# Two steps of one token block placed elsewhere in VectorE's queue, in a fused sketch-attention and SwiGLU kernel

## The chip, the cores and the metric

The kernel runs on one core of one Trainium2 chip. The metric is the device time of one execution in microseconds (us). The engines are named as in the profile: PE is TensorE, DVE is VectorE, ACT is ScalarE, POOL is GpSimd, SP is SyncE (here it only issues DMAs). Each engine works through its own queue of instructions strictly in order.

## What is computed

Two stages, in fp32. First, attention with sketched features, for 4 batches, 4 heads, 1088 tokens and 32 channels:

```
phi(x): a = S1 x, b = S2 x        (8 values each)
        phi = outer product of a and b, 64 features
kv  = sum over tokens of phi(k) v^T ;  z = sum over tokens of phi(k)
out = phi(q) kv / (phi(q) z + 1e-6)
```

The four heads of a token are put side by side (128 channels), which gives x with 4352 tokens. Second, a SwiGLU block with d_ff = 1536:

```
g = x @ w_gate ;  silu = g / (1 + exp(-g)) ;  out = (silu * (x @ w_val)) @ w_out
```

## The kernel before

**Tiling.** x is held transposed (xT, 128 channels on the partitions). The tokens of the first batch form blocks 0 to 2; the other 3264 tokens form seven blocks of up to 480 tokens, numbers 3 to 9, which the code calls `line`. The 1536 hidden columns are 12 pieces of 128. One *unit* is one block by one piece: the two products for gate and value, the SiLU on ACT, and the product of the two, which is stored as a row of `hidden`. Later a *down* step (`down`, L1039) multiplies that row by w_out and adds it up in PSUM; it runs about five units behind. Blocks 3 to 9 give 84 units, numbered y = 0 to 83. Units 0 to 11 are block 3, units 12 to 23 are block 4, and so on.

**Products in parts.** To save PE passes, a product can be made from rounded parts (fp32r) in place of a full fp32 product. For this, the tokens of a block are cut into three parts by `cut_tokens` (L867), in two steps. The first step puts x1 on ACT (L875, a rounded copy) and x0 on POOL (L876, the remainder). The second step puts xd on DVE (L880, made from x0 and x1). The weights are cut likewise by `cut_weights` (L834; its instructions show as L865). Units 0 to 19 cut the value product only; from unit 20 on (`GATES`) both products are cut. `cut_unit` (L959) issues, for one of the units 0 to 19, this: on PE the product with xd (L968) and the full gate product (L970), on ACT a scaled copy (L972), on PE the products with x1 and x0 (L978, L979), on DVE the sum (L980), on ACT the SiLU (L986), and on POOL the product into `hbuf` (L991).

**The order of the work.** There is no scheduler: the order of the source is the order of every queue. The loop over y (L1346 on) issues in each unit: a group of attention work on PE, if y is in `GROUPS`; the unit itself; down steps; the next part of the attention generator (`parts_of`, L1224); a part of the cut gate weights (L865); and at the end the token steps whose time has come (`token_steps`, L1336 to L1340). So a step listed under y stands at the end of unit y in each engine's queue.

**The attention of the later batches** (`attentions`, L608) is spread between the units. For batch index 2, the third batch, the group at unit 4 forms the key sums on PE (L381, L713), and the key sketches of the fourth batch (L347); `fold` (L590) then makes from the sums the third column of the sketch matrix s123 on DVE, in three instructions (L594, L598, L601), and `spread_out` (L718) turns the sums on DVE (L723) and has SP copy them to other partitions and load the next values. The group at unit 6 multiplies the queries with s123 on PE (`query_sketches`, L335) into PSUM banks 6 and 7. After that, DVE makes the features in pieces (L370) and turns them (L758) for the group at unit 20 (L776). The same work for the fourth batch has its fold in the group at unit 20 and its query sketches in the group at unit 22.

**PSUM banks** are taken by the rule "the one whose last taking is longest ago" (`bank`, L113), with bank 3 held for the accumulators of the down steps. A unit takes three of them, so the banks of one unit come round again two to three units later.

Of the kernel before, what the change touches and what calls it, by code (L numbers as in the profile page):

```python
# [19 lines left out]
def kernel(  # L20
# [38 lines left out]
    NCH = Dff // P  # L59
# [807 lines left out]
    def cut_tokens(i, engine=nc.gpsimd):  # L867

        t0, n = blocks[i]
        x = xT[:, t0 : t0 + n]  # L870
        x1, x0, xd = x_parts[i] = [
            apool.tile([P, WB], F32R, tag=tag, name=name, bufs=2)
            for tag, name in (("qb", "x1"), ("dT", "x0"), ("rd", "xd"))
        ]
        nc.scalar.activation(x1[:, 0:n], x, AF.Copy, scale=CUT)  # L875
        engine.tensor_tensor(  # L876
            out=x0[:, 0:n], in0=x, in1=whole(x1[:, 0:n]), op=ALU.subtract
        )
        yield
        nc.vector.scalar_tensor_tensor(  # L880
            out=xd[:, 0:n], in0=whole(x0[:, 0:n]), scalar=-BETA, in1=whole(x1[:, 0:n]),
            op0=ALU.mult, op1=ALU.add,
        )
# [452 lines left out]
    token_steps = {}  # L1336
    for m, i in enumerate(line[1:], 1):
        gen = cut_tokens(i)
        for at in {2: (20, 22), 3: (27, 32), 4: (40, 42)}.get(m, (NCH * m - 10, NCH * m - 9)):
            token_steps.setdefault(at, []).append(gen)  # L1340
    oldest[0] = True
    hold("acc")
# [71 lines left out]
```

## Time and profile before

| | us |
|---|---|
| median of 5 runs | 287.15 (287.02 to 288.04) |
| the profiled execution, whole | 286.94 |
| its span, first to last instruction | 285.1 |
| PE busy in it | 276.5 |
| DVE busy in it | 220.8 |
| unit 4 starts on PE (L968) | 101.89 |
| unit 6 starts on PE (L968) | 108.57 |
| unit 12 starts on PE (L968) | 121.87 |

The granted TensorE clock was 0.999 over the whole span. A profile line gives a line of the kernel (L880), an engine, an operation, and the tiles it writes and reads by their names without numbers (so x1, x0 and a unit's `x` all show as `x`). In a timeline the first two columns are the start and the duration in us; idle time of the engine ahead of the instruction stands in brackets, with the instruction that ended it. In the chain of work the columns are start, duration, and what worked. The records of two PE instructions that follow each other overlap[...].

### The profile page before, as it was taken

The page shows a single profiled execution, that of the slowest core. Times are in us where ns is not written, and L with a number is a line of the kernel's source. Part 1 is how long each engine was busy: PE and PEld are TensorE (multiplying, and loading weights), DVE is VectorE, ACT ScalarE, POOL GpSimd, SP SyncE. Part 2 cuts the span into 40 slices and gives each one's busy share as a digit, 9 for nine tenths or more (in the row PEclk, how much of TensorE's full clock was granted, in tenths as well). Part 3 has the DMA queues.
Part 4 walks back from the last instruction along what each step waited for, and adds up shares of the span by engine and source line. Part 5 has one row for each costly group of instructions (what it writes and reads, how often), then busy time and mean ns, then how long its engine had stood idle before and what let it go on. Part 6 is the DMA issues. An engine that isn't in the chain of part 4 may idle for free.

```text
span 285.1 us, 5583 instructions
## 1 busy us (share of the span) xinstructions
PE 276.5 (97%) x2129; PEld 191.1 (67%) x2129; DVE 220.8 (77%) x324; ACT 175.3 (62%) x316; POOL 177.3 (62%) x173
## 2 busy tenths in 40 slices
PE   7899999999999989999999999999999999999995
PEld 7545565667665656555576677757777777778984
DVE  3997988975495968998657898749889979988741
ACT  3468665723401846655366776867878888877760
POOL 3315432279500886589935787759879789878660
PEclk9999999999999999999999999999999999999999
DMA  6574194222321122000200020001000200010021
GB/s 196 158 220 112 51 273 132 80 78 80 79 44 28 26 80 78 17 0 2 34 18 0 0 36 2 0 2 22 13 0 1 37 0 0 10 28 1 0 35 28
DMA packets 26138, 14.28 MB, mean 50 GB/s; under 512 B 19840, under 2 KB 24192, under 8 KB 26112
## 3 DMA queue, kind: packets, MB, share of 16 engines
q1 hardware_dynamic: 25456, 13.84, 19.1%
q8 instruction: 16, 0.26, 0.4%
q10 hardware_dynamic: 656, 0.10, 0.2%
q14 instruction: 10, 0.08, 0.1%
HBM read 11.41 MB, written 2.23 MB: 48 GB/s over the span
## 4 chain that ended last, share of the span: by engine, by line
PE 89%; DVE 5%; DMA 1%; ACT 1%; POOL 1%; issue 1%; SPq 0%; DVEq 0%; ACTq 0%
PE PS L1060 24%; PE PS L1015 16%; PE PS L968 11%; PE PS L978 10%; PE PS L979 10%; PE PS L970 5%; PE PS L776 2%; PE PS L335 2%; PE PS L347 2%; PE PS L381 2%; DMA kld<-in_k_dram 1%; DVE xd L880 1%; PE PS L1088 1%; PE PS L1055 1%; PE PS L1054 1%; PE PS L1052 1%
## 5 line engine op out<-in xcount | busy, mean ns | idle before, releaser
L991 POOL TENSOR_TENSOR hbuf<-sg,sum 128x480 f32<-128x480 f32 (+1 forms) x83 | 105.3, 1273 | 37.5 <-ACT sg L986 29.2
L980 DVE SCALAR_TENSOR_TENSOR sum<-PS,sum 128x960 f32<-128x960 f32 (+2 forms) x83 | 83.2, 1003 | 26.6 <-ACT sum L972 21.7
L972 ACT ACTIVATE sum<-PS 128x960 f32<-128x960 f32 (+2 forms) x83 | 70.9, 854 | 39.3 <-PE PS L968 37.2
L1060 PE MATMUL PS<-hbuf,wo 128*128 128x480 f32 (+3 forms) x142 | 57.5, 505 | 0.0
L968 PE MATMUL PS<-xd,gphq 128*128 128x480 f32 (+1 forms) x63 | 40.1, 636 | 0.5 <-DVE xd L880 0.5
L978 PE MATMUL PS<-x,w 128*128 128x480 f32 (+1 forms) x83 | 38.5, 464 | 0.0
L986 ACT ACTIVATE sg<-sum 128x480 f32<-128x480 f32 (+1 forms) x63 | 36.6, 581 | 1.0 <-DVE sum L980 0.9
L968 PE MATMUL PS<-xd,wd 128*128 128x480 f32 (+1 forms) x83 | 35.8, 432 | 0.5 <-DVE xd L880 0.5
L1060 PEld LDWEIGHTS PS<-hbuf,wo 128*128 128x128 f32 x142 | 26.6, 189 | 8.4 <-issue 0.9
L979 PE MATMUL PS<-x,wb 128*128 128x480 f32 (+1 forms) x83 | 31.2, 376 | 0.0
L1015 PE MATMUL PS<-xT,wg 128*128 128x384 f32 (+1 forms) x74 | 29.5, 480 | 0.0
L1015 PE MATMUL PS<-xT,wv 128*128 128x384 f32 (+1 forms) x74 | 28.8, 471 | 0.2 <-DVE wv L279 0.2
L1019 ACT ACTIVATE sg<-PS 128x384 f32<-128x384 f32 (+1 forms) x31 | 14.4, 467 | 21.3 <-PE PS L1015 19.6
L968 PEld LDWEIGHTS PS<-xd,wd 128*128 128x128 f32 x83 | 15.7, 189 | 13.1 <-issue 11.4
L978 PE MATMUL PS<-x,graw 128*128 128x480 f32 (+1 forms) x63 | 23.5, 373 | 0.2 <-ACT xT L793 0.2
L979 PE MATMUL PS<-x,graw 128*128 128x480 f32 (+1 forms) x63 | 23.3, 370 | 0.0
L1060 PE MATMUL PS<-hbuf,scaled 128*128 128x480 f32 x48 | 23.2, 564 | 0.0
L1015 PEld LDWEIGHTS PS<-xT,wv 128*128 128x128 f32 x74 | 13.8, 190 | 9.2 <-DVE hbuf L1030 0.9
L968 PEld LDWEIGHTS PS<-xd,gphq 128*128 128x128 f32 x63 | 11.9, 188 | 11.7 <-issue 6.9
L1015 PEld LDWEIGHTS PS<-xT,wg 128*128 128x128 f32 x74 | 13.3, 189 | 9.3 <-issue 1.2
L978 PEld LDWEIGHTS PS<-x,w 128*128 128x128 f32 x83 | 15.6, 188 | 5.8 <-issue 3.4
L979 PEld LDWEIGHTS PS<-x,wb 128*128 128x128 f32 x83 | 15.6, 188 | 5.7 <-issue 4.3
(173 smaller groups left out, 457.1 us busy)
## 6 DMA issues: line engine op xcount, KB each, us to landing
kld<-in_k_dram SPq DMA_DIRECT2D x4, 544.0 KB, 4.2
vld<-in_v_dram SPq DMA_DIRECT2D x12, 144.0 KB, 5.2
qld<-in_q_dram SPq DMA_DIRECT2D x3, 544.0 KB, 3.4
raw<-in_moe_w_out_dram SPq DMA_DIRECT2D x4, 384.0 KB, 4.7
raw<-in_moe_w_gate_dram SPq DMA_DIRECT2D x3, 384.0 KB, 3.7
raw<-in_moe_w_val_dram SPq DMA_DIRECT2D x3, 384.0 KB, 3.5
out_dram<-o SPq DMA_DIRECT2D x16, 60.0 KB, 2.0
vld<-in_v_dram SPq DMA_DIRECT2D x4, 112.0 KB, 4.1
```

Of the source, the lines that this page charges most:

```text
L335: nc.tensor.matmul(ps[32 * a : 32 * a + 32, 96 * (c - c0) : 96 * (c - c0) + 96], qT[:, 4 * c + a, :], s123[:, a : a + H, :, :].rearrange(" ...
L968: nc.tensor.matmul(ds[:, k], wd, xd, start=True, stop=True)
L970: nc.tensor.matmul(g, wg[:, j, :], xT[:, t0 : t0 + n], start=True, stop=True)
L972: nc.scalar.activation(sums, ds, AF.Copy, scale=-1.0 / BETA)
L978: nc.tensor.matmul(ps[:, k], w1, x1, start=True, stop=False)
L979: nc.tensor.matmul(ps[:, k], wb, x0, start=False, stop=True)
L980: nc.vector.scalar_tensor_tensor(out=sums, in0=ps, scalar=1.0 + 1.0 / BETA, in1=sums, op0=ALU.mult, op1=ALU.add)
L986: nc.scalar.activation(sg, sums[:, 0] if both else g, AF.Silu)
L991: nc.gpsimd.tensor_tensor(out=hj[:, 0:n], in0=sg, in1=sums[:, len(ws) - 1], op=ALU.mult)
L1015: nc.tensor.matmul(o[:, 0:n], w[:, j, :], xT[:, t0 : t0 + n], start=True, stop=True)
L1019: nc.scalar.activation(sg[:, 0:n], g[:, 0:n], AF.Silu)
L1060: nc.tensor.matmul(acc[i][:, 0:n], w, hidden[i, j][:, 0:n], **sides)
```

## The change

The steps of block m of `line` were listed under the units 12m - 10 and 12m - 9, unless given by hand. For m = 1, block 4, that is units 2 and 3. The change gives this block a pair by hand, units 3 and 8:

```
 for m, i in enumerate(line[1:], 1):
     gen = cut_tokens(i)
-    for at in {2: (20, 22), 3: (27, 32), 4: (40, 42)}.get(m, (NCH * m - 10, NCH * m - 9)):
+    for at in {1: (3, 8), 2: (20, 22), 3: (27, 32), 4: (40, 42)}.get(m, (NCH * m - 10, NCH * m - 9)):
         token_steps.setdefault(at, []).append(gen)
```

So x1 and x0 of block 4 stand at the end of unit 3 in the queues of ACT and POOL, where they stood at the end of unit 2, and xd of block 4 stands at the end of unit 8 in DVE's queue, where it stood at the end of unit 3, ahead of the fold of the third batch. Block 4 is first used in unit 12. Nothing else is changed.

More of the change, by code (lines that the diff above doesn't have):

```diff
@@ L1338 @@
         gen = cut_tokens(i)
-        for at in {2: (20, 22), 3: (27, 32), 4: (40, 42)}.get(m, (NCH * m - 10, NCH * m - 9)):
+        for at in {1: (3, 8), 2: (20, 22), 3: (27, 32), 4: (40, 42)}.get(m, (NCH * m - 10, NCH * m - 9)):
             token_steps.setdefault(at, []).append(gen)
```

## The prediction

> **What bounds the kernel now.** I read the page first, to see which engine holds the end.
>
> ```profile
> span 285.1 us, 5583 instructions
> PE 276.5 (97%) x2129; PEld 191.1 (67%) x2129; DVE 220.8 (77%) x324; ACT 175.3 (62%) x316; POOL 177.3 (62%) x173
> ```
>
> TensorE (PE) is busy for 97% of the span, and 89% of the chain that ended last is PE. So a change on VectorE (DVE), ScalarE (ACT) or GpSimd (POOL) counts only if it takes away, or adds, a wait of PE. The view of waits, for PE alone, lists all of them; its columns are the total, the number and the longest, in us.
>
> ```profile
> PE PS L335 <- DVE spread L723: 1.1, 1, 1.1
> PE PS L968 <- DVE xd L880: 1.0, 2, 0.5
> ```
>
> The first is one single stall, the longest of the kernel. The chain of work in order of time (start, duration, what) tells what lies behind it.
>
> ```profile
> 103.21 1.17 POOL x L876
> 104.40 1.64 DVE xd L880
> 106.04 0.15 DVE fold L594
> ...
> 106.66 0.25 DVE spread L723
> 106.95 1.69 PE PS L335 x72
> ```
>
> In order: POOL makes x0 of block 4, DVE makes xd of block 4 from it, then come the sums of the third batch (fold, L594 to L601) and the turn of its sums (L723), then PE's query sketches (L335). The fold needs nothing of block 4: it stands behind xd only because DVE works in order. Its own inputs were there long before: PE's last matmul for it (L713) began at 100.17 and took 0.29 us, so about 100.5. DVE's own timeline shows the queue before and after that place (start, us; the idle time in brackets).
>
> ```profile
> 101.14 0.99 DVE L865 TENSOR_TENSOR late<-wg,graw 128x384 f32<-128x384 f32 x1
> ...
> 115.09 0.64 DVE L980 SCALAR_TENSOR_TENSOR sum<-PS,sum 128x480 f32<-128x480 f32 x1
> 115.66 0.94 DVE L370 TENSOR_TENSOR late<-kab 128x768 f32<-128x768 f32 x1
> 116.53 1.56 DVE L865 SCALAR_TENSOR_TENSOR gphq<-late,graw 128x384 fp32r<-128x384 f32 x1
> 118.02 0.64 DVE L980 SCALAR_TENSOR_TENSOR sum<-PS,sum 128x480 f32<-128x480 f32 x1
> ...
> 121.26 0.65 DVE L980 SCALAR_TENSOR_TENSOR sum<-PS,sum 128x480 f32<-128x480 f32 x1
> ...
> 128.55 0.66 DVE L980 SCALAR_TENSOR_TENSOR sum<-PS,sum 128x480 f32<-128x480 f32 x1 [0.16 <-PE PS L979]
> ...
> 130.79 0.66 DVE L980 SCALAR_TENSOR_TENSOR sum<-PS,sum 128x480 f32<-128x480 f32 x1 [0.70 <-PE PS L979]
> ...
> 133.10 0.66 DVE L980 SCALAR_TENSOR_TENSOR sum<-PS,sum 128x480 f32<-128x480 f32 x1 [0.35 <-PE PS L979]
> ```
>
> DVE is idle from 102.13 to 104.40 (2.26 us, released by POOL's x). From unit 6's sum at 110.41 on it has no gap until 128.55. The new place of xd is in this dense stretch: behind L865 at 116.53, ahead of unit 9's sum at 118.02. PE's timeline gives what L335 costs with and without a wait.
>
> ```profile
> 104.91 0.97 PE L1060 MATMUL PS<-hbuf,wo 128*128 128x480 f32 x2
> 106.95 1.69 PE L335 MATMUL PS<-s,qT 128*32 128x96 f32 x72 [1.07 <-DVE spread L723]
> 146.03 0.97 PE L1060 MATMUL PS<-hbuf,wo 128*128 128x480 f32 x2
> 146.93 1.69 PE L335 MATMUL PS<-s,qT 128*32 128x96 f32 x72
> ```
>
> The same pair of lines stands 0.90 us apart in the fourth batch (146.03 to 146.93) and 2.04 here: 1.14 us are stall by this reading, 1.07 by the bracket.
>
> **The change part by part.** No instruction is added or removed: one ACT instruction (x1, L875), one of POOL (x0, L876) and one of DVE (xd, L880) stand later in their queues. The step issues no DMA.
>
> *Taken away: xd ahead of the fold.* After the change DVE comes from L865, which ends at 102.13, straight to the fold. Its four instructions take 0.21, 0.27, 0.22 and 0.24 us; from the fold's start to the transpose's end they took 106.90 - 105.97 = 0.93 us, so they end at about 103.1. PE wants L335 at 104.91 + 0.90 = 105.81. That leaves 2.7 us of cover, so the whole stall goes: -1.07 to -1.14 us, I take -1.1. What is late next at this place? L335 also needs its PSUM banks, 6 and 7. Followed through the code's oldest-bank rule, bank 6 held the third batch's sums (read by the fold and the transpose, 103.1) and bank 7 unit 4's first product (read by ACT at 102.42, 0.57 us long). Its queries were turned by 99.5. Nothing is late.
>
> A rule of the Trainium skill speaks against this cover. "SBUF — State Buffer", section "Who interferes with whom", has it that a VectorE instruction with two SBUF inputs and a GpSimd one that reads SBUF exclude each other for a whole instruction. The row agrees: xd took 1.64 us at 104.40, beside POOL's product at 104.32 (1.21 us), and 0.65 us at 92.36. Of the four, L601 alone has two SBUF inputs; moved to 102.6 it meets POOL's products, which run without a gap from 99.01. By the plain row (0.22) the sums end at 103.1; by the rule, waiting out a whole product, 1.2 us later, 104.3. That is still 1.5 us ahead of 105.81, so both give the same sum.
>
> *Moved: x1 on ACT, from unit 2 to unit 3.* It ran at 98.25 for 0.59 us and now follows the weight part of 99.64, so it ends by about 100.8. ACT was idle for 1.07 us before 101.24, so this costs nothing; without that idle time the copy there would be late by at most 0.6, and PE only sees it through banks reused two units later.
>
> *Moved: x0 on POOL, from behind unit 2's product to behind unit 3's.* 1.2 us each way: unit 3's product is earlier by that, x0 ends at about 105.6 instead of 104.4. Unit 4's product, which POOL started at 107.59 after 2.06 us of idle time, can start then. Cost nothing; its reader xd now stands some 11 us later.
>
> *Moved: SP's queue.* The six copies of spread and the load of the fourth batch's values wait for L723, which comes about 3.8 us earlier. They start near 103 instead of 106.97 and are needed at unit 20 (142): no cost, no gain.
>
> *Added: xd at unit 8's end.* It no longer waits. Queued behind it on DVE are unit 9's sum, two products of the features (L370), L865 and unit 10's sum. Its size lies between 0.65 us (alone) and 1.64 us (beside a POOL product). By the lock rule a whole extra wait is possible; but POOL's last product there (115.88, 1.80 us) ends at 117.68, ahead of xd at 118.02, and the next needs unit 9's sum, which is behind xd. So I take 0.65, with 1.64 for the range. In times of before (all now 1.1 earlier, PE and DVE alike):
> - Unit 12 needs xd at 121.87. It ends at 118.67 (119.66): 3.2 us (2.2) to spare.
> - Unit 13's first product reuses the bank of unit 10's sum. That ends at 121.91 + 0.65 = 122.56 (123.55); PE's record starts at 124.14: 1.6 us (0.6) to spare.
> - The idle gaps of DVE, 0.16, 0.70 and 0.35, swallow 1.21 us by unit 17, and 1.11 us more before unit 19's sum; the transposed features of the third batch, done at 138.76, are later by 0 (0.43) and needed at 140.50.
> - POOL follows its DVE sums. Its gap of 3.68 us ahead of 145.56 takes up the rest, and the products are read by PE five units later.
>
> So it adds no wait of PE; if this cover were gone, xd would cost its own 0.65 to 1.64 us.
>
> *Sum.* The profiled execution took 286.94 us (span 285.1 and 1.84 around it). 286.94 - 1.1 = 285.84. The median of the five runs, 287.15, is 0.21 above it; the same subtraction gives 286.05. After L335 the chain is PE all the way, but for the stall at 153.54 (0.51), which hangs on unit 22's own products and moves along. I add no gain there.
>
> **The rivals.** *Forecast (0.76): 286.05*, from 285.7 to 286.4.
>
> *Part of the gain (0.08): about 286.6.* The sums of the third batch lose more to POOL than one product, or the dense stretch costs 0.5 us at unit 13. For it: L865 took 0.54 us free and 1.0 to 1.3 beside POOL. Against it: 1.5 us spare at the first place and 0.6 at the second, both at their worst ends.
>
> *The wait is only renamed (0.08): 287.15.* If another input of L335 came last at 106.9, removing xd gains nothing. Against it: the bank and the queries above are all done by 104.3.
>
> *Slower (0.08): about 288.1.* The mechanism is VectorE's backlog between unit 8 and unit 13. If xd takes 1.64 and the insertion shifts the phase so that three of the now free instructions behind it also meet POOL (1.0 us each, the difference of xd's two rows), DVE is 4.6 us late at unit 10's sum. Unit 13's first product is held from where the lag passes 2.2 us (124.14 - 121.91), so PE loses 2.4, less the 1.1 won: +1.3, or 288.4; counted from the end of the matmul ahead in the chain (124.67) it is +0.7, or 287.9. I take 288.1. It turns the sign from a lag of about 3.3 us. Against it: only four POOL products fall into these units, and two of the instructions behind xd already pay for one.
>
> **How the numbers follow.** About 0.2% (0.57 us) is what a measurement of this kernel can tell from no change: faster is below 286.58, slower above 287.72. Faster: the forecast and half of the part gain, 0.80. Within: the other half and the renamed wait, 0.12. Slower: 0.08. The range from 285.6 to 286.9 holds the forecast and the part gain, 0.84.
>
> **What would show it.** In the profile after, L335 at unit 6 should have no wait and start 0.90 us after the L1060 ahead of it; the fold should start near 102.2; DVE's idle time before xd should be gone, with xd near 117 and 0.65 us long; unit 13's L968 should show no wait; the stall near 152.4 should still be 0.5; and the span about 284.0. I am wrong if L335 waits for another releaser, or if a new wait of PE for unit 10's sum, for xd at unit 12 or for phT at unit 20 appears.

## The result, and the profile after

The changed kernel takes 285.91 us (median of 24 runs, 285.49 to 287.68), the kernel before 287.12 us beside it. The ratio is 0.9965, with a 95% interval of 0.9954 to 0.9975: between 0.7 and 1.3 us faster. The forecast was 286.05.

The span is the better measure of a step of this size: what lies around it was 1.84 us in the profiled execution of before and 286.86 - 284.0 = 2.9 us in that of after, which hides the gain in the whole time of these two executions. Here are the first lines of the page of the changed kernel.

```profile
span 284.0 us, 5583 instructions
PE 277.0 (98%) x2129; PEld 191.3 (67%) x2129; DVE 220.6 (78%) x324; ACT 175.3 (62%) x316; POOL 177.2 (62%) x173
```

The span fell by 1.1 us; the number of instructions is the same, and no engine but PE changed its busy time by more than 0.2 us. Next, all waits of PE in the changed kernel that the view lists at 0.4 us or more (total, number, longest).

```profile
PE PS L968 <- DVE xd L880: 1.0, 2, 0.5
PE PS L234 <- PEq L1398: 0.9, 1, 0.9
PE PS L490 <- ACT kvz L1208: 0.4, 1, 0.4
```

The wait of L335 for DVE's transpose is gone and no other has come in its place. PE's timeline shows the same pair of lines as before:

```profile
104.95 0.97 PE L1060 MATMUL PS<-hbuf,wo 128*128 128x480 f32 x2
105.85 1.69 PE L335 MATMUL PS<-s,qT 128*32 128x96 f32 x72
```

They are 0.90 us apart, as in the fourth batch; before it was 2.04. DVE's timeline shows both places, the old and the new:

```profile
101.19 0.99 DVE L865 TENSOR_TENSOR late<-wg,graw 128x384 f32<-128x384 f32 x1
102.10 0.21 DVE L594 TENSOR_TENSOR fold<-PS,sq 128x64 f32<-128x64 f32 x1
102.35 0.27 DVE L598 TENSOR_REDUCE w<-fold 128x8 f32<-128x64 f32 x1
102.65 0.68 DVE L601 TENSOR_TENSOR s<-w,own 128x64 f32<-128x64 f32 x1
103.25 0.24 DVE L723 STREAM_TRANSPOSE spread<-PS 128x64 f32<-128x64 f32 x1
...
115.46 1.56 DVE L865 SCALAR_TENSOR_TENSOR gphq<-late,graw 128x384 fp32r<-128x384 f32 x1
116.94 0.65 DVE L880 SCALAR_TENSOR_TENSOR xd<-x,x 128x480 fp32r<-128x480 f32 x1
117.51 0.64 DVE L980 SCALAR_TENSOR_TENSOR sum<-PS,sum 128x480 f32<-128x480 f32 x1
...
120.76 0.64 DVE L980 SCALAR_TENSOR_TENSOR sum<-PS,sum 128x480 f32<-128x480 f32 x1
...
130.26 1.99 DVE L370 TENSOR_TENSOR phq<-qab 128x768 f32<-128x768 f32 x1
```

The fold starts straight behind L865 and its chain ends at 103.49. xd runs at 116.94 for 0.65 us, behind L865 and ahead of unit 9's sum. Two things are longer than I took them: L601 (0.68 us) and the feature product at 130.26 (1.99 us); more on them below.

### The profile page after: what moved, and what is told of

Its sections match the earlier page's. It is cut to its first block, busy times and chain, and to the rows that moved or that the text cites. A ratio compares the mean times of both kernels' runs of the same rounds, so it can differ in the third digit from the quotient of the medians.

```text
span 284.0 us, 5583 instructions
## 1 busy us (share of the span) xinstructions
PE 277.0 (98%) x2129; PEld 191.3 (67%) x2129; DVE 220.6 (78%) x324; ACT 175.3 (62%) x316; POOL 177.2 (62%) x173
## 4 chain that ended last, share of the span: by engine, by line
PE 89%; DVE 5%; ACT 2%; DMA 2%; issue 1%; SPq 0%; DVEq 0%; ACTq 0%
PE PS L1060 24%; PE PS L1015 16%; PE PS L968 11%; PE PS L978 10%; PE PS L979 10%; PE PS L970 5%; PE PS L776 2%; PE PS L335 2%; PE PS L347 2%; DMA kld<-in_k_dram 2%; PE PS L381 1%; DVE sum L980 1%; PE PS L1088 1%; PE PS L1055 1%; PE PS L1054 1%
## 5 line engine op out<-in xcount | busy, mean ns | idle before, releaser
L1060 PE MATMUL PS<-hbuf,wo 128*128 128x480 f32 (+3 forms) x142 | 57.5, 505 | 0.0
L1060 PEld LDWEIGHTS PS<-hbuf,wo 128*128 128x128 f32 x142 | 26.6, 189 | 8.4 <-issue 0.9
L1060 PE MATMUL PS<-hbuf,scaled 128*128 128x480 f32 x48 | 23.2, 564 | 0.0
```

The costliest lines, as they stand in the source:

```text
L1060: nc.tensor.matmul(acc[i][:, 0:n], w, hidden[i, j][:, 0:n], **sides)
```

## The experiments

The theory: PE's stall was a queueing accident. The fold stood on DVE behind xd, and xd waited for POOL's x0. The rivals: moving x1 and x0 makes part of the gain; xd's own time is what costs; unit 8 is a special place; the cover in the dense stretch is thin. All "before" times are medians of runs beside the experiment on the same chip, 287.06 to 287.09 us.

A measure that the start of the kernel doesn't touch helps to read them, since the profiled executions start PE's units up to 2 us apart (the first keys come at a different time, and the first product on them, L347, took 1.49 us in before and 2.19 in the kernel with xd three times). It is the time from the start of unit 4's group (L381) to the query sketches of unit 6 (L335), and from there to the numerators of unit 20 (L776), all starts taken from PE's timelines:

| kernel | steps at | L381 to L335 | L335 to L776 | ratio to before (95%) |
|---|---|---|---|---|
| before | 2, 3 | 7.81 | 33.55 | 1 |
| after | 3, 8 | 6.64 | 33.54 | 0.9965 (0.9954 to 0.9975) |
| xd alone moved | 2, 8 | 6.64 | 33.54 | 0.9952 (0.9935 to 0.9968) |
| x0 alone moved | 3, 3 | 8.00 | 33.54 | 1.0013 (1.0002 to 1.0023) |
| x0 early | 0, 3 | 6.66 | 33.55 | 0.9958 (0.9944 to 0.9972) |
| xd at 4 | 2, 4 | 6.64 | 33.54 | 0.9979 and 0.9947, see below |
| xd three times | 3, 8 | 6.67 | 33.54 | 0.9962 (0.9946 to 0.9978) |
| xd seven times | 3, 8 | 6.64 | 35.81 | 1.0051 (1.0032 to 1.0071) |
| xd at 11 | 3, 11 | 6.63 | 39.94 | 1.0147 (1.0121 to 1.0172) |
| the same, PE kept busy | 3, 11 | 6.63 | 37.05 | 1.0062 (1.0041 to 1.0084) |

**One half of the change at a time.** First xd alone.

```
-... in {1: (3, 8), 2: (20, 22), ...
+... in {1: (2, 8), 2: (20, 22), ...
```

> Steps at units 2 and 8: xd alone is moved, x1 and x0 stay. Queue theory (the fold stood behind xd, and xd behind POOL's x0): the whole gain, about -1.1 us against before, L335 of unit 6 without a wait. Rival (the earlier room on ACT and POOL from moving x1 and x0 makes part of it): clearly less than -1.1, down to 0.

Measured 285.84 us against 287.06, a gain of 1.2; L335 has no wait. The rival falls: moving x1 and x0 is not needed. Then x1 and x0 alone.

```
+... in {1: (3, 3), 2: (20, 22), ...
```

> Steps at units 3 and 3: x1 and x0 alone are moved, xd stays ahead of the fold. Queue theory: x0 ends on POOL at about 105.6 and xd, alone by then, at 106.3, so L335 waits until 107.2: about +0.2 us against before, wait of PE about 1.3. Rival (moving x1 and x0 makes part of the gain): below before by some tenths or more.

Measured 287.41 us against 287.06. By the ratio that is +0.4 us (0.1 to 0.7), by the table's first interval +0.19. PE's two longest waits in this kernel:

```profile
PE PS L335 <- DVE spread L723: 1.3, 1, 1.3
PE PS L968 <- DVE xd L880: 1.0, 2, 0.5
```

The stall became longer, as x0 became later. This half of the change works, by itself, in the wrong direction.

**The wait or the work?** Here xd stays where it was before, ahead of the fold, but its input is made earlier.

```
+... in {1: (0, 3), 2: (20, 22), ...
```

> Steps at units 0 and 3: xd stays where it was in before, ahead of the fold, but x0 is made on POOL three units' products earlier, so that xd need not wait. Queue theory: xd starts at about 102.1, takes 0.65 to 1.64 us, the fold's chain ends at 103.7 to 104.8, ahead of 105.81: about -1.1 us, though xd still stands first. Rival (xd's own time in front of the fold is what costs, not its wait for POOL): the gain is smaller than -1.1 by 0.65 to 1.64 us.

Measured 285.94 us against 287.06. DVE's timeline of this kernel:

```profile
102.41 1.66 DVE L880 SCALAR_TENSOR_TENSOR xd<-x,x 128x480 fp32r<-128x480 f32 x1
103.99 0.21 DVE L594 TENSOR_TENSOR fold<-PS,sq 128x64 f32<-128x64 f32 x1
...
105.14 0.24 DVE L723 STREAM_TRANSPOSE spread<-PS 128x64 f32<-128x64 f32 x1
```

xd is at its slowest (1.66 us), it is still ahead of the fold, and nothing is lost: the chain ends at 105.38, and PE's L335 began at 106.15 without a wait, 0.89 us behind the L1060 ahead of it. So the wait for POOL was the cost; xd's own time fits under the cover.

**Is unit 8 a special place?** xd goes right behind the fold and unit 4's sum.

```
+... in {1: (2, 4), 2: (20, 22), ...
```

> Steps at units 2 and 4: xd right behind the fold and unit 4's sum, ahead of the dense stretch. Queue theory: about -1.1 us against before, the same as the change; xd runs between 105 and 106.5, in DVE's idle time, and nothing of the stretch from unit 8 on is later than in before. Rival (unit 8 is needed): a stall of PE at unit 6 or later, less than -1.1.

The profile had the full gain, span 283.9, but the median was 286.53 against 287.08 (ratio 0.9979, 0.9966 to 0.9992). Since profile and times disagreed, it ran again beside the changed kernel.

> Steps at units 2 and 4 again, beside the changed kernel on the same chip: its profile had the full gain (span 283.9) but its times lay only 0.55 us below before. Queue theory: the same as the changed kernel within 0.2 us. Rival (the place at unit 4 gives part of the gain away): above the changed kernel by 0.3 to 0.6 us.

> The changed kernel again, as the measure for the others of this call: -1.1 us against before.

Measured 285.93 us for xd at unit 4 (ratio 0.9947, 0.9929 to 0.9966) and 286.02 for the changed kernel (0.9955, 0.9937 to 0.9973), against 287.09. The two are the same. The first median was high because of what lies around the span, over 2.2 us in 9 of its 22 runs (2 of 34 of before): the median of their spans, 284.15, was 1.15 below that of before. Unit 8 has no merit of its own.

**How thin is the cover in the dense stretch?** The changed kernel, with xd of block 4 written several times:

```
+        for _ in range(3 if i == 4 else 1):     # 7 in the second
             nc.vector.scalar_tensor_tensor(out=xd[:, 0:n], ...
```

> The changed kernel, with xd of block 4 written three times at unit 8 (the same values), so DVE's lag at unit 10's sum is about 1.95 us in place of 0.65. Spare time as reckoned (1.6 us left at unit 13's bank, 3.2 at unit 12): no new wait of PE, still -1.1 us against before. Rival (the cover in the dense stretch is thinner than reckoned): a new wait of PE of up to 1.3 us.

Measured 285.99 us against 287.08, and no new wait of PE: two more instructions on DVE, 1.3 us of them, cost nothing. From the first xd to unit 9's sum it was 1.94 us in this trace.

> The changed kernel, with xd of block 4 written seven times at unit 8 (the same values): a lag of about 4.55 us at unit 10's sum. Backlog theory (PE is held from a lag of 2.2 us on): PE loses 1.8 to 2.4 us, in units 12 and 13: +0.7 to +1.3 us against before. Rival (other slack takes it up, such as idle time of DVE in units 15 to 19): nearer to -1.1.

Measured 288.82 us against 287.08, by the ratio +1.5 us (0.9 to 2.0). The waits of PE in this kernel (its lines are one further on: L969 is the unit's first product, L981 the sum):

```profile
PE PS L969 <- DVE sum L981: 1.8, 2, 1.1
PE PS L969 <- DVE xd L881: 1.0, 2, 0.5
```

The first line is new: units 12 and 13 wait for the banks of the sums of units 9 and 10. In the table PE loses 35.81 - 33.54 = 2.27 us, within the 1.8 to 2.4 expected, at 4.72 us from the first xd to unit 9's sum. So the rival that would have made this change slower is real, and needs a lag of more than 1.9 us, where xd alone causes about 0.6.

**As late as it can stand.**

```
+... in {1: (3, 11), 2: (20, 22), ...
```

> Steps at units 3 and 11: xd as late as it can stand. Backlog theory (DVE has no gap here, so the place inside the stretch matters): xd follows unit 11's sum and the dot of the queries, ends at about 123.9, and unit 12's first product, wanted at 120.8, waits 3.1 us: about +2.0 us against before. Rival (DVE has time enough anywhere once the fold is ahead): -1.1 us.

Measured 291.02 us against 287.06: +4.0, twice what was expected. The wait itself came out as reckoned, 3.14 us at unit 12. PE's timeline shows what came on top of it:

```profile
119.18 0.96 PE L970 MATMUL PS<-xT,wg 128*128 128x480 f32 x2
...
124.52 0.77 PE L968 MATMUL PS<-xd,wd 128*128 128x480 f32 x1 [3.14 <-DVE xd L880]
125.08 1.80 PE L970 MATMUL PS<-xT,wg 128*128 128x480 f32 x2
125.95 1.33 PE L978 MATMUL PS<-x,w 128*128 128x480 f32 x1
...
131.34 0.97 PE L1060 MATMUL PS<-hbuf,wo 128*128 128x480 f32 x2
```

The same two products L970 take 0.96 us ahead of the wait and 1.80 behind it. A view of stretches agrees (the length, then the busy us of PE, PEld (PE's weight loads), DVE, ACT and POOL with counts, then the granted clock, the DMA share and GB/s):

```profile
116.00:121.00 5.00, 5.00 (x17) 2.73 (x15) 5.00 (x7) 2.98 (x6) 2.21 (x2) 1.00 0.00 0
121.00:125.00 4.00, 0.86 (x2) 0.48 (x2) 3.43 (x5) 0.00 (x0) 3.93 (x3) 0.86 0.00 0
125.00:129.00 4.00, 4.00 (x8) 2.01 (x7) 1.12 (x3) 1.14 (x2) 0.97 (x2) 0.50 0.00 0
129.00:133.00 4.00, 4.00 (x12) 2.32 (x10) 2.51 (x3) 1.57 (x3) 2.85 (x3) 0.79 0.00 0
133.00:137.00 4.00, 4.00 (x14) 2.35 (x13) 2.52 (x5) 1.85 (x4) 4.00 (x4) 1.00 0.01 2
```

The granted clock is 0.50 from 125 to 129, and full again from 133. To tell this from other costs of the stall, PE was given 16 small products to do while it waits, in the kernel with xd at unit 11.

```
+        if y == 12:
+            keep_warm(16, w=480, ps=ds[:, 0])
         for k, (_, _, wd) in enumerate(parts):
             nc.tensor.matmul(ds[:, k], wd, xd, start=True, stop=True)
```

> The kernel with xd at unit 11, and 16 small bf16 products (480 columns each) put on PE ahead of unit 12's first product, written into a bank that this product overwrites: they fill the 3.1 us in which PE waited for xd. Clock theory (the loss of 4.0 us against before, twice what was expected, is the wait of 3.4 us less the 1.1 won, plus a granted clock of 0.50 in the 4 us behind the wait): no dip of the clock, about +2.3 us against before. Rival (the extra time is in waits of DVE and POOL behind the stall): still +3.5 to +4.

Measured 289.3 us against 287.09, by the ratio +1.8 us (1.2 to 2.4), by the medians +2.2. The clock stayed at 1.00 in all three stretches from 121 to 133, of which this is the middle one:

```profile
125.00:129.00 4.00, 4.00 (x15) 2.35 (x13) 2.51 (x5) 2.29 (x4) 2.25 (x3) 1.00 0.00 0
```

Unit 12's first product starts as late as without the small products (124.56 for 124.52), but the clock is not the same: by the table the two profiled executions differ by 39.94 - 37.05 = 2.9 us, the medians of the two sets of runs, on two chips, by 1.7.

**The same accident in two other places.** The changed kernel still has two waits of PE for an xd, of 0.5 us each. One is block 5's, at unit 24, behind unit 22's sum and the dot of the fourth batch.

```
-... in {1: (3, 8), 2: (20, 22), ...
+... in {1: (3, 8), 2: (20, 21), ...
```

> The changed kernel, with block 5's second step at unit 21 in place of 22, so that its xd stands ahead of the wait for unit 22's sum and of the dot of the fourth batch. If the 0.49 us that PE waits at unit 24 for this xd is the same kind of queueing: the wait is gone, about 0.5 us below the changed kernel, -1.6 against before. Rival (the sum of unit 22 or a bank is late as well and takes its place): no gain over the changed kernel.

Measured 285.03 us against 287.08 (ratio 0.9923, 0.9903 to 0.9944). DVE's timeline:

```profile
146.60 1.22 DVE L880 SCALAR_TENSOR_TENSOR xd<-x,x 128x480 fp32r<-128x480 f32 x1
149.48 1.16 DVE L980 SCALAR_TENSOR_TENSOR sum<-PS,sum 128x960 f32<-128x960 f32 x1 [1.66 <-ACT sum L972]
```

xd now lies in what was idle time of DVE, 2.79 us before and 1.66 now. From the fourth batch's query sketches to the start of PE's last record of L1088 it takes 132.79 us where the changed kernel takes 133.55: 0.76 less, for a wait recorded as 0.49 (the lines are at the end). The other is block 3's, at unit 0, behind three feature products. Both of its steps are now issued together.

```
         if begun[0]:
             x_steps = x_steps or cut_tokens(HEAD, nc.vector)
-            next(x_steps, None)
+            run(x_steps)
```

> The kernel with block 5's second step at unit 21, and block 3's two steps issued together, so that its xd stands ahead of the first features of the third batch on DVE instead of behind them. If the wait of PE at unit 0 (0.46 us) is queueing of the same kind: xd ends near 91.1, the wait goes, and the features and POOL's sums behind them end 0.65 us later, at about 99.7, where unit 4's group wants them at 99.4 by then: -0.4 to -0.75 us against that kernel. Rival (the group's sums come late and the wait only moves there): no gain.

Measured 284.1 us against 287.09 (ratio 0.9882, 0.9861 to 0.9903). This is 0.9 us below the kernel with block 5 at unit 21 (medians of two sets of runs, with before at 287.08 and 287.09), a little more than the 0.4 to 0.75 expected. The longest waits of PE in it:

```profile
PE PS L234 <- PEq L1398: 0.9, 1, 0.9
PE PS L490 <- ACT kvz L1208: 0.4, 1, 0.4
```

No wait for an xd is left. With the three moves together the kernel is 3.0 us, 1.2%, faster than before, and no instruction was added or removed.

## Why the prediction was right

**The stall.** The prediction reckoned 1.07 by the bracket and 1.14 from start to start, and took 1.1. The interval from L381 to L335 fell by 7.81 - 6.64 = 1.17 us; part of the profiled span's gain is taken back by PE's first unit starting 0.07 later (93.23 for 93.16). Start to start was the better reading. The cause is shown, not only argued: xd alone moved gives the gain, x0 alone moved makes the stall longer, and x0 made earlier gives the gain with xd in its old place.

**The lock rule at L601.** The row said 0.22, the rule of the Trainium skill ("SBUF — State Buffer", section "Who interferes with whom"), as the prediction used it, up to a whole POOL product more. L601 took 0.68 us. The rule held, but its price was the rest of the product that was running, not a whole one: POOL had begun it at 101.73 and took 1.52 us, so 0.60 us of it were left at 102.65, and L601 ended 0.08 after it, ahead of most of POOL's next product. The same reading gives xd's slow row in before: POOL's product ended at 104.32 + 1.21 = 105.53, and xd 0.51 later. The sum didn't depend on it, since the chain ended at 103.49 and PE wanted it at 105.85.

**xd at unit 8.** Taken at 0.65 with 1.64 as the far end; it took 0.65, at 116.94, after POOL's product had ended (116.60) and before the next began (118.30). Its two neighbours fit the order reckoned, and unit 13's first product had no wait.

**The features of the third batch.** Here a size was off. I had the last transpose (L758) later by 0, at most 0.43, by subtracting DVE's idle gaps. It ended at 137.28 + 0.96 = 138.24; in before it ended at 138.76, which moved by 1.1 is 137.66. So it was later by 0.6. Two feature products (L370, one of them the line at 130.26) took 1.99 us where they had taken 1.38 and 1.40. Here is the first of them in before, in the changed kernel, and with xd at unit 4, with the POOL instruction that it meets (in the third run POOL's instruction began at 129.50 and took 1.28 us).

```profile
130.66 1.28 POOL L540 TENSOR_TENSOR zs<-zs 128x512 f32<-128x512 f32 x1
131.37 1.38 DVE L370 TENSOR_TENSOR phq<-qab 128x768 f32<-128x768 f32 x1
...
130.15 1.29 POOL L540 TENSOR_TENSOR zs<-zs 128x512 f32<-128x512 f32 x1
130.26 1.99 DVE L370 TENSOR_TENSOR phq<-qab 128x768 f32<-128x768 f32 x1
...
130.21 1.38 DVE L370 TENSOR_TENSOR phq<-qab 128x768 f32<-128x768 f32 x1
```

In each, L370 ends 0.81 us after POOL's instruction: it waits for the rest, 0.57 us in before and 1.18 after. DVE had taken up its lag in its idle gaps (131.37 - 1.1 = 130.27, and L370 starts at 130.26), but POOL had not (130.66 - 1.1 = 129.56, and L540 starts at 130.15). With xd at unit 4 nothing is added to the dense stretch, and L370 takes 1.38. So xd's 0.6 us came back by way of POOL. It cost nothing, because L776 was wanted only at 139.39. But idle gaps had been counted as if durations were fixed.

**The slower rival** was sized right as far as the runs go: the prediction let it start at a lag of 2.2 us, the runs place its start between a reckoned lag of 1.95 (free) and one of 4.55 (which costs 2.27). What I didn't name is that unit 12 waits as well, for the bank of unit 9's sum, with 3.2 us to spare in before.

**Readings that were off without effect.** L723 came 3.4 us earlier, not 3.8, for L601 was longer; x0 took 1.56 us and ended at 105.95, not 105.6; L865 beside POOL reaches 1.56 us (at 116.53), not 1.3; and the copies of spread are read from 140.50 on (L776), not 142. The stall at 153.54 was put down to unit 22's own products; the run with block 5 at unit 21 shows that it hung on the place of xd in DVE's queue.

**The place.** The change needed only "behind the fold, and early enough". Nothing in the runs favours unit 8 over unit 4.

## What to carry to other kernels

When an engine that is not the bound stalls the one that is, look at what stands ahead of the late instruction in its in-order queue, and whether that has to be there; moving it costs nothing if its own deadline and the lag behind it are reckoned. Take the size of a stall from starts, not from the idle time in brackets: from the start of the instruction ahead of the wait to that of the one behind the late instruction, less the same distance at a place without the wait. A lag that one engine takes up in its idle gaps can live on in another that follows it. And let a move be tested by its halves: one half of this change did all of it, the other was slightly harmful alone.

## What was not expected of the hardware

A wait of PE can cost more than its length. In the kernel with xd at unit 11 PE's last product ahead of the wait ended at 121.39. The granted clock fell to 0.50 at about 123.9, while PE still waited, and stayed there until about 130.7, 6.2 us after PE had taken up work at 124.52 (its mean is 0.95 from 123 to 124, 0.50 from 124 to 130 and 0.64 from 130 to 131). The products took 1.80 us in place of 0.96; with small products in that wait the clock stayed at 1.00. Two of the timed runs of that kernel had a span of 290.4 us and a mean clock of 0.988, three had 288.8 to 288.9 and 0.993; by an estimate from these means (the share of the clock that is missing, times the span, over 0.5) that is about 7 and 4 us at half clock, so the price differs from run to run. Two waits of 1.07 and 0.72 us, in the kernel with xd seven times, did not lower it: every slice of the page's row of granted clock is a 9. The Trainium skill has such a rule ("TensorE: Matmul & The Clock Gate", Part 1, the clock gate: half clock after an idle window of about 3.4 us, full clock after as long a busy one). The 0.50 agrees with it; the two lengths do not: here the clock fell after 2.5 us without a product, and came back after 6.2 us of work. Its worth was 2.9 us in the profiled executions and 1.7 by the medians, beside a wait of 3.14.

A wait recorded as 0.49 us, taken away, was worth 0.76 us, and one of 1.07 was worth 1.17. Here are the lines for the first, in the changed kernel and with block 5's second step at unit 21:

```profile
150.96 0.97 PE L1060 MATMUL PS<-hbuf,wo 128*128 128x480 f32 x2
152.42 0.48 PE L968 MATMUL PS<-xd,gphq 128*128 128x480 f32 x1 [0.49 <-DVE xd L880]
152.74 0.38 PE L968 MATMUL PS<-xd,wd 128*128 128x480 f32 x1
...
151.19 0.96 PE L1060 MATMUL PS<-hbuf,wo 128*128 128x480 f32 x2
151.62 0.76 PE L968 MATMUL PS<-xd,gphq 128*128 128x480 f32 x1
152.22 0.38 PE L968 MATMUL PS<-xd,wd 128*128 128x480 f32 x1
```

The record of a matmul that has waited starts later and is shorter (0.48 for 0.76 us of the same product), while without a wait its record overlaps that of the product before it. So the bracket is too small, and the distance to the late product's own start too large (1.46 - 0.43 = 1.03); up to the start of the product behind it, 1.78 - 1.03 = 0.75 is right.
